# A recurrent-memory attention kernel: four streaming slots and 45 resident weight granules in place of five and 44

## The chip, the core and the metric

The kernel runs on one core of a Trainium2 chip. The metric is device time in microseconds (us) of one launch, as the median of several runs. Each weight that the kernel needs more than once has either to stay in SBUF, the on-chip memory of the core, or to be fetched again from HBM, the chip's main memory.

The engines are named as in the profile: PE (TensorE, matrix products), PEld (its weight loads), DVE (VectorE), ACT (ScalarE), POOL (GpSimd) and SP (SyncE, which here only issues transfers). DMA means the core's 16 transfer engines. "Granted clock" is the share of full speed that the chip let TensorE run at.

## The reference

The input `x` (2048 rows of 1024, bfloat16) is normalized by rows. The result is the sum of `x`, a recurrent attention layer, and a small routed layer:

```python
for s in range(64):                       # 2048 rows in segments of 32
    h = concatenate([mem, xn[32*s:32*s+32]])         # 8 memory rows + 32 rows
    q, k, v = h @ Wq, h @ Wk, h @ Wv                 # each 1024 -> 32 heads x 128
    p = softmax(where(mask, q @ k.T * 128**-0.5, -1e9))
    o = (p @ v) @ Wo                                 # 4096 -> 1024
    mem = o[:8]                                      # goes into the next segment
    outs.append(o[8:])
out = x + concatenate(outs) + B(xn)
```

`o` of a segment has 40 rows: the first 8 become the memory of the next one, so the 64 segments run strictly one after another. `B` scores all rows with one vector, takes the two best rows, sends only those through a gated layer (1024 to 3584 and back), and adds the result to these two rows.

## The kernel before

**Granules.** The four matrices Wq, Wk, Wv, Wo hold 32 MB in bfloat16, of which the kernel keeps only a part in SBUF. It cuts them into 64 granules of 128 x 2048 elements (512 KB): granules 0 to 47 are six phases of eight (`PHASES`: Q first half, K first half, Q second half, K second half, V first half, V second half; eight granules sum over the 1024 inputs), and granules 48 to 63 are Wo, two heads in each. Every segment uses all 64 in this order.

**Resident and streamed.** 44 granules (`N_RES`) are loaded once, in the first segment, and stay in SBUF (tiles `wres`). The other 20 are streamed: in the first segment from the input, and copied at the same time (`copy_block`, by POOL's queue) into a contiguous scratch array in HBM (`wsc`); in each of the 63 later segments they are fetched from there (`fetch`, L327 on SP's queue) into one of `N_SLOT` = 5 slots (tile `g`) that are used in turn. The streamed granules are 2, 5, 6, 9, 13, 17, 21, 25, 29, 33, 36, 39, 41, 44, 47, 50, 53, 56, 59, 62. Two are special: granule 6 (`KEPT_WHOLE`) lies in PSUM after the first segment and is never fetched again (ACT and DVE copy it back into small tiles in each segment), and of granule 25 (`KEPT_PART`) only the first half is fetched; the other half is copied from PSUM into its slot by two DVE copies (`kept_piece`, L354), which are hooked behind granules 17 and 18 in the order of DVE. So a later segment fetches 18 whole granules and one half.

**What starts a fetch.** SP takes its transfers in the order written. A fetch into a slot waits until PE has done the last matrix product that reads the granule five fetches earlier, which had the same slot. Landing is a second condition on PE's side: a product with a streamed granule waits until its fetch has landed. Nothing else paces the fetches.

**PE's order.** PE takes its products in the order written. For a granule of Q, K, V it does four products side by side (L661, tile `PSm`), for one of Wo eight (L713, tile `WO`). Each segment's 24 first rows (with the 8 memory rows) go through this main pass. The 8 rows that remain of each segment are gathered over four segments and go through the weights as a "left" pass of 32 rows (L644 and the `WL` products of L713): Q and K for the next group in segments j = 1 and 2 of a group of four, V in segment j = 0, Wo in segment j = 3 and partly the start of the next one. So a granule is read a second time in some of the segments, right behind the main product (in the second V phase of j = 0 the reads of its first granules wait until the fourth; in Wo of j = 3, those of granule 48 until granule 49), and its slot is free only then.

**Other paths.** Between the phases ACT copies a phase's sums out of PSUM (`XB`, `VM`), PE transposes them back (L515), DVE copies K's (`KT`, L525), and scores, softmax and the weighted sums follow at fixed places among the granules. After the last granule of a segment the eight memory rows are turned (`mem_to_st`) and the next segment starts.

**Start and end.** In the first segment SP loads granules, resident and streamed, and the tiles of `x` for the row statistics, about 14 granules ahead of PE. In the last segment every resident tile becomes free after its use, and SP fetches the 46 tiles of the routed layer into them and into the slots (`fetch_moe`, tiles `MW`), behind the last streamed fetch. Its products (L858, L871) end the kernel.

Of the kernel before, what the change touches and what calls it, by code (L numbers as in the profile page):

```python
# [14 lines left out]
PSUM = bass.MemoryType.PSUM  # L15
DRAM = bass.MemoryType.DRAM

N_RES = 44
N_SLOT = 5
KEPT_WHOLE = 6  # L20
KEPT_PART = 25
LEFT_OUT = 35
NEG = -30000.0

PHASES = [(0, 0), (1, 0), (0, 1), (1, 1), (2, 0), (2, 1)]
# [3 lines left out]
def kernel(  # L29
# [41 lines left out]


    NG = 64
    n_str = NG - N_RES
    streamed = [((2 * i + 1) * NG) // (2 * n_str + 2) for i in range(n_str + 1)]
    streamed.remove(LEFT_OUT)

    moved = {1: 2, 4: 5, 7: 9, 10: KEPT_WHOLE, 16: 17, 19: 21, 22: KEPT_PART, 25: 29, 28: 33, 32: 36, 38: 39}
    streamed = sorted(moved.get(g, g) for g in streamed)
    resident = [g for g in range(NG) if g not in streamed]  # L80

    def granule_dram(g):
# [13 lines left out]
    front = ctx.enter_context(tc.tile_pool(name="front", bufs=1, reuse_waits="tile"))  # L96
    wstream = ctx.enter_context(tc.tile_pool(name="wstream", bufs=N_SLOT))
    one = ctx.enter_context(tc.tile_pool(name="one", bufs=1, reuse_waits="tile"))
# [10 lines left out]
    def columns(g, s):  # L109
        if s > 0 and g == KEPT_WHOLE:  # L110
            return None
        return slice(0, 1024 if s > 0 and g == KEPT_PART else 2048)

# [190 lines left out]
    def new_stl(t):  # L304
# [10 lines left out]
    KEPT_COLS = {KEPT_WHOLE: {0: KEPT[0][:, 0:512], 1: KEPT[0][:, 512:1024], 2: KEPT[1][:, 0:512], 3: KEPT[1][:, 512:1024]},  # L315
                 KEPT_PART: {2: KEPT[2][:, 0:512], 3: KEPT[2][:, 512:1024]}}

    def fetch():
        if not flow:
            return  # L320
        s, g = flow.pop(0)
        t = wstream.tile([P, 2048], BF16, tag="g", name="g")
        c = columns(g, s)
        if s == 0:
            nc.sync.dma_start(out=granule_out(t, g), in_=granule_dram(g))
        elif c is not None:
            nc.sync.dma_start(out=t[:, c], in_=wsc[g][:, :])  # L327
        queued.append((g, t))
# [19 lines left out]
    def bring_back(c, copy):  # L348
        back[c] = one.tile([P, 512], BF16, tag=("bx", "bE", "kt", "bC")[c], name="BK")
        copy(out=back[c][:, :], in_=KEPT_COLS[KEPT_WHOLE][c])  # L350

    def kept_piece(g, c, copy):
        t = [t for q, t in queued if q == g][0]
        copy(out=t[:, 512 * c:512 * (c + 1)], in_=KEPT_COLS[g][c])  # L354
# [16 lines left out]
    def fetch_moe():  # L371
        while moe and free_homes:
            what = moe.pop(0)
            h = free_homes.pop(0)
            t = home(h, [P, 2048], BF16, "MW") if h >= 0 else wstream.tile([P, 2048], BF16, tag="g", name="g")
            if what[0] == "gu":
                _, w, kc, fh = what
                nc.sync.dma_start(out=t[:, 0:FH],
                                  in_=(B_w_gate, B_w_up)[w][kc * P:(kc + 1) * P, FH * fh:FH * (fh + 1)])
            else:  # L380
                nc.sync.dma_start(out=t.rearrange("p (a d) -> p a d", a=2),
                                  in_=B_w_down[2 * what[1] * P:(2 * what[1] + 2) * P, :].rearrange("(a p) d -> p a d", a=2))
            moe_tiles[what] = t
# [19 lines left out]
    for g in range(48):  # L403
        if g in streamed:
            n_q += 1
            if n_q < N_SLOT:
                fetch()
            continue
        if n_q >= N_SLOT:
            break  # L410
# [89 lines left out]
    for s in range(NSEG):  # L500
# [8 lines left out]
        def hook(p, kc, fn):  # L509
            hooks.setdefault((p, kc), []).append(fn)  # L510
# [112 lines left out]
        if s > 0:  # L623
            hook(0, 0, lambda: bring_back(3, nc.scalar.copy))
            hook(2, 1, lambda: kept_piece(KEPT_PART, 2, nc.vector.tensor_copy))
            hook(2, 2, lambda: kept_piece(KEPT_PART, 3, nc.vector.tensor_copy))
            hook(1, 5, turn_lx)
# [20 lines left out]
        for p, (mat, half) in enumerate(PHASES):  # L648
# [8 lines left out]
            for kc in range(KC):  # L657
                g = 8 * p + kc
# [140 lines left out]

    free_homes += [-1] * N_SLOT  # L800
    fetch_moe()
# [111 lines left out]
```

## Time and profile before

| what | value |
|---|---|
| median of 3 runs | 1981.58 us (1977.93 to 1991.66) |
| the profiled execution, its own time | 1977.82 us |
| its span, first to last instruction | 1976.2 us |
| PE busy | 1633.7 us (83%) |
| DMA moved | 712.43 MB, mean 361 GB/s |
| mean granted TensorE clock | 0.953 |

The profile page gives for each engine how long it was busy, then the span in 40 slices, the DMA queues, the chain of work that ended last, and groups of instructions. A "group" row names the line of the kernel, the engine, the operation, the tile written and the tiles read, the count, and what the engine waited for just before it. The view of windows gives the same busy times for stretches of the span that one chooses, with the mean granted clock, the share of time that the 16 DMA engines were busy, and the rate. The view of waits says which engine stood idle until what ended it: total us, number of times, longest one.

### The profile page before, as it was taken

What the parts mean: (1) busy time and instruction counts of PE and PEld (TensorE: products, weight loads), DVE (VectorE), ACT (ScalarE), POOL (GpSimd) and SP (SyncE); (2) the same over time, 40 slices, a digit from 0 to 9 for tenths busy, and PEclk for the clock granted to TensorE, in tenths of its full rate; (3) what the DMA queues carried; (4) which work ended last, traced back from release to release, by engine and by line L of the source; (5) the groups of instructions that cost most, each with busy time, mean ns of one, the idle gap of its engine ahead of it and who ended that gap; (6) DMA issues with size and microseconds to landing.
All of it is one profiled execution on the core that took longest, in us unless ns stands there. A gap on an engine that the chain in (4) does not pass through costs nothing.

```text
span 1976.2 us, 82904 instructions
## 1 busy us (share of the span) xinstructions
PE 1633.7 (83%) x36080; PEld 891.5 (45%) x36080; DVE 884.4 (45%) x2848; ACT 730.5 (37%) x1995; POOL 439.7 (22%) x882
## 2 busy tenths in 40 slices
PE   3558888988888898889898888888888898988863
PEld 1224544444454444445454544445444444544443
DVE  6724544454444434443453445444444544444430
ACT  1123343434334343433343444433434343343320
POOL 3201213112221312222121312222132122212110
PEclk8669999999999999999999999999999999999995
DMA  9999999999999999999999999999999999999998
GB/s 368 405 337 365 355 361 359 375 354 353 373 344 368 365 359 375 347 379 340 362 352 352 380 365 376 343 364 350 350 349 357 370 347 361 348 354 361 375 387 335
DMA packets 232124, 712.43 MB, mean 361 GB/s; under 512 B 39296, under 2 KB 53168, under 8 KB 231760
## 3 DMA queue, kind: packets, MB, share of 16 engines
q1 hardware_dynamic: 194384, 671.18, 91.5%
q0 software_dynamic: 28736, 28.09, 4.4%
q10 hardware_dynamic: 8640, 7.87, 1.1%
q8 instruction: 282, 4.62, 0.9%
q14 instruction: 82, 0.67, 0.1%
HBM read 694.32 MB, written 22.29 MB: 363 GB/s over the span
## 4 chain that ended last, share of the span: by engine, by line
DMA 47%; PE 40%; DVE 4%; ACT 3%; issue 3%; POOL 2%; SPq 1%; ACTq 0%; POOLq 0%; DVEq 0%
DMA g<-wsc 36%; PE PSm L661 18%; PE WO L713 7%; PE PSl L644 5%; DMA out_dram<-OL 4%; PE BT L515 3%; PE WL L713 2%; POOL out_dram L792 1%; PE BT L465 1%; DMA MW<-in_B_w_gate_dram 1%; DVE XR L227 1%; DMA MW<-in_B_w_up_dram 1%; ACT QT L520 1%; DMA ql_d<-XBl 1%; DMA g<-in_A_Wq_dram 1%
## 5 line engine op out<-in xcount | busy, mean ns | idle before, releaser
L661 PE MATMUL PSm<-wres,ST 128*32 128x512 bf16 x8448 | 723.0, 387 | 15.7 <-DVE ST L282 5.4
L661 PEld LDWEIGHTS <-ST 128*32 128x32 bf16 x12288 | 325.7, 96 | 420.9 <-issue 195.1
L661 PE MATMUL PSm<-g,ST 128*32 128x512 bf16 x3588 | 367.6, 389 | 108.5 <-DMA g<-wsc 89.0
L677 ACT CAST XB<-PSm 128x512 bf16<-128x512 f32 x256 | 150.5, 588 | 306.5 <-PE PSm L661 306.5
L713 PEld LDWEIGHTS <-OT 128*32 128x32 bf16 x8192 | 205.3, 98 | 114.7 <-issue 90.9
L713 PE MATMUL WO<-wres,OT 128*32 128x256 bf16 x5632 | 237.0, 282 | 22.3 <-issue 13.8
L458 POOL DMA_DIRECT2D LX<-ql_d x63 | 33.5, 532 | 910.8 <-DVE OTL L592 325.9
L644 PE MATMUL PSl<-wres,STL 128*32 128x512 bf16 x2112 | 203.1, 391 | 13.4 <-ACT VL L701 12.4
L525 DVE COPY KT<-BT 128x512 bf16<-128x512 bf16 x128 | 53.3, 416 | 321.0 <-issue 163.0
L252 POOL DMA_DIRECT2D XN<-in_A_x_dram x256 | 128.4, 507 | 244.1 <-DMA out_dram<-XN 126.7
L778 POOL DMA_DIRECT2D out_dram<-XN x256 | 129.1, 513 | 233.0 <-DVE XN L776 227.4
L713 PE MATMUL WO<-g,OT 128*32 128x256 bf16 x2560 | 133.6, 283 | 41.3 <-DMA g<-wsc 29.0
L644 PEld LDWEIGHTS <-STL 128*32 128x32 bf16 x3072 | 85.1, 98 | 74.5 <-issue 26.3
L515 PE MATMUL BT<-IDENT,XB 128*128 128x128 bf16 x1024 | 102.0, 222 | 17.9 <-ACT XB L677 16.3
L697 ACT CAST VM<-PSm 128x512 bf16<-128x512 f32 x128 | 79.2, 619 | 100.5 <-PE PSm L661 100.5
L515 PEld LDWEIGHTS <-XB 128*128 128x128 bf16 x1024 | 58.4, 98 | 124.1 <-ACT XB L677 83.5
L354 DVE COPY g<-KEPT 128x512 bf16<-128x512 bf16 x126 | 47.6, 419 | 143.7 <-PE PSm L661 85.9
L542 DVE TENSOR_TENSOR BS<-BS,CT 128x96 f32<-128x96 f32 (+1 forms) x256 | 59.6, 233 | 101.0 <-PE BS L535 96.6
L583 PEld LDWEIGHTS <-VM 32*128 32x128 bf16 x2048 | 69.6, 92 | 77.9 <-issue 72.2
L520 ACT COPY QT<-BT 128x512 bf16<-128x512 bf16 x128 | 75.2, 588 | 71.1 <-PE BT L515 64.8
L552 ACT ACTIVATE BS<-BS 128x320 f32<-128x320 f32 x128 | 54.1, 423 | 116.9 <-DVE BS L548 116.8
L644 PE MATMUL PSl<-g,STL 128*32 128x512 bf16 x900 | 93.2, 391 | 0.0
(171 smaller groups left out, 2435.2 us busy)
## 6 DMA issues: line engine op xcount, KB each, us to landing
g<-wsc SPq DMA_DIRECT2D x1134, 512.0 KB, 6.0
g<-wsc SPq DMA_DIRECT2D x63, 256.0 KB, 5.5
LX<-ql_d POOLq DMA_DIRECT2D x63, 128.0 KB, 6.1
MW<-in_B_w_gate_dram SPq DMA_DIRECT2D x16, 448.0 KB, 9.2
MW<-in_B_w_up_dram SPq DMA_DIRECT2D x16, 448.0 KB, 9.0
wres<-in_A_Wk_dram SPq DMA_DIRECT2D x12, 512.0 KB, 12.3
MW<-in_B_w_down_dram SPq DMA_DIRECT2D x12, 512.0 KB, 10.4
wres<-in_A_Wq_dram SPq DMA_DIRECT2D x11, 512.0 KB, 11.4
```

Source lines behind the costliest of these rows:

```text
L252: nc.gpsimd.dma_start(out=XN[32 * g:32 * g + XM, :], in_=x2[s * SEG:s * SEG + XM, 256 * g:256 * (g + 1)])
L515: nc.tensor.transpose(out=PTq[:, il, :, :].rearrange("p j r -> p (j r)"), in_=XB[:, il * P:(il + 1) * P], identity=IDENT[:, :])
L520: nc.scalar.copy(out=QT[half][:, :, :], in_=pv)
L542: nc.vector.tensor_tensor(out=S4, in0=S4, in1=m, op=ALU.add)
L552: nc.scalar.activation(out=S8, in_=S8, func=ACTF.Exp, scale=SCALE)
L583: nc.tensor.matmul(o, lhsT=VM[half][q0:q0 + 32, il * P:(il + 1) * P], rhs=PTm[q0:q0 + 32, il, 0:NK], start=True, stop=False, tile_position ...
L644: nc.tensor.matmul(PSl[32 * jq:32 * jq + 32, :], lhsT=STL[:, g % KC, :], rhs=part(Gv, jq), start=first_, stop=last_, tile_position=(0, 32 ...
L661: nc.tensor.matmul(PSm[32 * jq:32 * jq + 32, :], lhsT=ST[:, kc, :], rhs=part(Gv, jq), start=(kc == 0), stop=(kc == KC - 1), tile_position= ...
L677: nc.scalar.copy(out=XB[:, :], in_=PSm[:, :])
L697: nc.scalar.copy(out=VM[half][:, :], in_=PSm[:, :])
L713: nc.tensor.matmul(PS[32 * g:32 * g + 32, 0:256], lhsT=lhs(h), rhs=Gv[:, D * hs + 256 * g:D * hs + 256 * (g + 1)], start=False, stop=(last ...
L778: nc.gpsimd.dma_start(out=out2[s * SEG:s * SEG + XM, 256 * g:256 * (g + 1)], in_=OB[32 * g:32 * g + XM, :])
```

## The change

The kernel keeps 45 granules resident in place of 44 and streams 19 in place of 20. The room for the additional resident granule is that of a slot: there are four slots in place of five, so a fetch now waits for the granule four fetches earlier. A later segment fetches 17 whole granules and one half.

The list of streamed granules is written out in place of the formula. It becomes 2, 4, 6, 9, 13, 17, 21, 24, 29, 34, 36, 39, 42, 45, 48, 51, 55, 59, 62: 5 gives way to 4, 25 to 24, 33 to 34, 41, 44, 47, 50, 53, 56 to 42, 45, 48, 51, 55. The granule that is kept in part in PSUM is 24 in place of 25. Granule 48, the first one of Wo, is now streamed. Everything else in the file is the same; lines behind the list move up by three.

```diff
-N_RES = 44
-N_SLOT = 5
+N_RES = 45
+N_SLOT = 4
 KEPT_WHOLE = 6
-KEPT_PART = 25
-LEFT_OUT = 35
+KEPT_PART = 24
...
     NG = 64
-    n_str = NG - N_RES
-    streamed = [((2 * i + 1) * NG) // (2 * n_str + 2) for i in range(n_str + 1)]
-    streamed.remove(LEFT_OUT)
-
-    moved = {1: 2, 4: 5, 7: 9, 10: KEPT_WHOLE, 16: 17, 19: 21, 22: KEPT_PART, 25: 29, 28: 33, 32: 36, 38: 39}
-    streamed = sorted(moved.get(g, g) for g in streamed)
+
+    streamed = [2, 4, KEPT_WHOLE, 9, 13, 17, 21, KEPT_PART, 29, 34, 36, 39, 42, 45, 48, 51, 55, 59, 62]
+    assert len(streamed) == NG - N_RES
+    n_str = len(streamed)
     resident = [g for g in range(NG) if g not in streamed]
```

## The prediction

> **What bounds the kernel now.** I read the page first: span, engines, DMA queues, the chain that ended last and the DMA issues.
>
> ```profile
> span 1976.2 us, 82904 instructions
> PE 1633.7 (83%) x36080; PEld 891.5 (45%) x36080; DVE 884.4 (45%) x2848; ACT 730.5 (37%) x1995; POOL 439.7 (22%) x882
> ...
> DMA  9999999999999999999999999999999999999998
> ...
> q1 hardware_dynamic: 194384, 671.18, 91.5%
> ...
> DMA g<-wsc 36%; PE PSm L661 18%; PE WO L713 7%; PE PSl L644 5%; DMA out_dram<-OL 4%; PE BT L515 3%; PE WL L713 2%; POOL out_dram L792 1%; PE BT L465 1%; DMA MW<-in_B_w_gate_dram 1%; DVE XR L227 1%; DMA MW<-in_B_w_up_dram 1%; ACT QT L520 1%; DMA ql_d<-XBl 1%; DMA g<-in_A_Wq_dram 1%
> ...
> g<-wsc SPq DMA_DIRECT2D x1134, 512.0 KB, 6.0
> g<-wsc SPq DMA_DIRECT2D x63, 256.0 KB, 5.5
> ```
>
> The reader is to see two busy resources side by side: the DMA engines are at nine tenths or more nearly everywhere, PE is busy for 83%, and the chain changes between PE and the streamed fetches (1134 whole, 63 half: 18 and 1 in each of 63 segments). The windows and the waits of PE say how near the two are.
>
> ```profile
> 155.00:1908.00 1753.00, 1526.39 (x34105) 832.41 (x34104) 790.21 (x2598) 696.64 (x1913) 400.41 (x796) 0.98 0.98 360
> 0.00:105.00 105.00, 46.84 (x578) 20.59 (x578) 71.65 (x180) 14.46 (x35) 27.98 (x64) 0.77 1.00 388
> 1908.00:1976.00 68.00, 28.64 (x863) 23.48 (x862) 5.52 (x22) 7.23 (x17) 6.62 (x12) 0.65 0.91 350
> ```
>
> ```profile
> PE PSm L661 <- DMA g<-wsc: 89.0, 153, 1.6
> PE WO L713 <- DMA g<-wsc: 29.0, 67, 1.7
> ```
>
> ```profile
> L705 PE MATMUL WO<-XS,IDENT x64: 269/269/393, 104.9 to 1908.5; 128*128 128x256 bf16 x64
> ```
>
> The last three figures of a window are granted clock, DMA share and GB/s. L705 runs once a segment, so it marks the segments; the long window holds 62 of them, 1753 / 62 = 28.3 us each. In it DMA works for 0.98 x 28.3 = 27.7 us a segment. PE stands for streamed data for 89.0 + 29.0 = 118 us in 220 waits, 0.54 us in each and 118 / 63 = 1.9 us a segment; without them a segment would take 26.4 us. **The bound is the stream**, with PE and what it waits for otherwise only 1.3 us behind.
>
> The four kinds of segment differ. I took one group of four without any fall of the clock (1.00), whose sum, 113.3 us, is near four average segments (113.1), cut at the marks of L705, and its waits on streamed data: none in the first stretch, then those below.
>
> ```profile
> 549.13:580.82 31.69, 27.42 (x666) 16.48 (x666) 13.69 (x48) 11.08 (x33) 9.60 (x18) 1.00 0.93 327
> 580.82:607.58 26.76, 24.28 (x540) 12.72 (x540) 12.05 (x38) 12.33 (x35) 4.73 (x10) 1.00 0.99 360
> 607.58:635.10 27.52, 24.37 (x538) 12.85 (x537) 12.44 (x41) 11.50 (x33) 4.71 (x10) 1.00 1.00 369
> 635.10:662.46 27.36, 21.69 (x474) 11.48 (x473) 12.66 (x43) 10.31 (x31) 7.17 (x14) 1.00 1.01 385
> ```
>
> Second stretch:
>
> ```profile
> PE PSm L661 <- DMA g<-wsc: 0.9, 2, 0.5
> ```
>
> Third, then fourth:
>
> ```profile
> PE WO L713 <- DMA g<-wsc: 1.4, 3, 0.9
> PE PSm L661 <- DMA g<-wsc: 1.2, 3, 0.5
> ```
>
> ```profile
> PE PSm L661 <- DMA g<-wsc: 2.2, 4, 0.7
> PE WO L713 <- DMA g<-wsc: 1.7, 3, 1.2
> ```
>
> DMA work (length x share) is 29.5, 26.5, 27.5, 27.6 us; the length without these waits is 31.7, 25.9, 24.9, 23.5 us. The larger of each pair adds up to 31.7 + 26.5 + 27.5 + 27.6 = 113.3, the measured sum. So in this group five slots carry the stream to its bound: no time is lost beside the larger of the two.
>
> **The change part by part.** *One whole fetch less in each of 63 segments.* Queue q1 moved 671.18 MB in 91.5% of the span, 1808 us, so a granule (0.524 MB) costs 1808 / 671.18 x 0.524 = 1.41 us of all engines. It takes 63 x 1.41 = 89 us of DMA work out, and once the 0.5 MB copy into `wsc`, 1.4 us at the same rate, in the first 105 us (DMA 1.00). Not all 89 us come back, because PE is next. In the group above DMA work falls to 28.1, 25.1, 26.1, 26.2, the other side stays, and the larger of each pair adds up to 31.7 + 25.9 + 26.1 + 26.2 = 109.9: 3.4 to 3.5 us a group, 0.87 a segment, **55 us** in all, if four slots carried the stream as well as five.
>
> *One slot less.* A fetch starts one streamed granule later.
>
> ```profile
> L327 SPq DMA_DIRECT2D g<-wsc x1197: 319/320/1618, 119.0 to 1908.4; - x200
> ...
> DMA to landing us min/median/max: 3.2/6.0/10.6
> ```
>
> A slot turns in 5 x 28.3 / 19 = 7.45 us: 6.0 in flight, 1.45 landed and not yet released. With four slots and 18 fetches it has 4 x T / 18, at 28.3 us 6.3 us. If the flight stayed at 6.0 and the hold fell to about 0.5 (a product, 0.38, and SP), T would be 18 x 6.5 / 4 = 29.3 us, against 27.4 with full gain. But most of the flight is queueing behind the kernel's own fetches: the fastest of 1197 landed in 3.2 us, and half a granule less moves the median by 0.5 us (5.5 against 6.0), so one whole granule less ahead should take about 1.0 off: 5.0 in flight, which an even flow bears easily (18 x 5.5 / 4 = 24.8 us). What the slot guarded against is an uneven flow: the reserve over the shortest turn (3.2 + 0.5 = 3.7 us, 2.6 granules at 1.41) falls from 2.4 granules to 1.4. Bounds: nothing at the one end; at the other 29.3 - 27.4 = 1.9 us a segment. I take one more average wait in each segment, 0.54 us, **34 us** in all, since the waits are the nearest row for a buffer run dry: now 3.5 a segment with a reserve of 2.4.
>
> [...]
>
> *The new places.* Counts of PE, DVE and ACT instructions stay; the products only read other tiles. In segments that end a group, granule 48's slot comes free only at granule 49, at most about 0.4 us later (26.4 / 64 a granule) in 16 segments: bounds 0 and 7 us, taken at 0, since its successor 62 is 14 granules away. In the second V phase 42 replaces 41 among the granules whose release waits for the fourth; that is no worse.
>
> *The kept half.* The two copies into the slot now wait for granule 9's release in place of 5's, and K's copy is queued behind them on DVE, with the scores (L533) behind that.
>
> ```profile
> L354 DVE COPY g<-KEPT x126: 411/420/426, 136.2 to 1891.7; 128x512 bf16<-128x512 bf16 x126
> ```
>
> ```profile
> PE BS L533 <- DVE KT L525: 6.8, 19, 0.6
> ```
>
> From granule 9 to 19, where K's copy is due, PE needs 10 x 0.41 = 4 us, against 0.84 us for both copies. I take 0; if this cover were gone, 63 times the longest wait, 0.6, is 38 us.
>
> *Start and end.* Fetch 9 goes out behind more resident loads; in the first 105 us DMA is at 1.00, so order changes nothing but who waits: 0. The end is the routed layer's 46 tiles, in 45 homes and a slot, behind the last streamed fetch:
>
> ```profile
> 1899.16 6.87 DMA g<-wsc
> ...
> 1912.19 9.26 DMA MW<-in_B_w_gate_dram
> ...
> 1970.07 0.62 PE YP L871 x8
> ```
>
> The same bytes follow the same event: 0.
>
> **Sum**: -55 + 34 - 1 = -22 us. The profiled execution, 1977.8 us (span and 1.6 around it), goes to 1956; on the median, 1981.6, which is 3.8 above it, to **1959**, 1.1% faster.
>
> **The rivals.** *A, the lost slot costs nothing*: 55 + 1 us gained, 1925. For it: the group above loses nothing with five, and fetches land sooner with fewer bytes queued. Against: the reserve nearly halves. *B, the flight does not shrink*, and the stream is bound by four slots: T = 29.3 us, 63 x (29.3 - 28.3) = +63 us, 2044. It decides where flight and hold exceed 4 x 28.3 / 18 = 6.29 us, that is, a median landing of 5.8. For it: landings up to 10.6 us. Against: DMA is at 0.98, so flight is mostly queue. In part (landing near 5.9) it gives 1990 to 2000. *C, even*: two more average waits a segment (68 us), 1994, or 1.6 of them, 1980. *D, other waits take the place of the removed ones*:
>
> ```profile
> PE BT L515 <- ACT XB L677: 16.3, 26, 1.2
> PE PSl L644 <- ACT VL L701: 12.4, 13, 2.4
> ```
>
> Where PE comes sooner, ACT's copies end later than it: at twice these rows 29 us less gain, beside the 34, which is 1988. *E, the clock*: the shallower buffer bunches waits, as here after three in a row:
>
> ```profile
> 999.70:1006.50 6.80, 6.80 (x122) 3.17 (x122) 3.44 (x16) 2.03 (x10) 0.00 (x0) 0.50 0.98 377
> ```
>
> A mean of 0.98 is 4% of the stage, 70 us, at half speed; were it 8%, 35 us of PE time would go, half of it on the path where PE binds: 1959 + 18 = 1977. [...]
>
> That the change doesn't do what it says is unlikely: the count of fetches follows from the list.
>
> **How the numbers follow.** Forecast 0.44 (1940 to 1970); A 0.24 (1915 to 1940); C, D and E together 0.18 (1970 to 1995); B 0.14 (1995 to 2044). A change of 1% (20 us) is about what a measurement of this kernel tells from none, its runs lying between 1978 and 1992. Faster by over 1% (under 1962): all of A and two thirds of the forecast, 0.53. Slower by over 1% (over 2001): most of B, 0.13, and 0.02 of the rest. Same 0.32. The range leaves out the low part of A and B's: 1922 to 1996.
>
> **What would show it.** Fetches 1071 whole and 63 half; q1 near 638 MB; median landing near 5.0 us, where 5.8 or more is B; DMA share near 0.94 in the long window, 27.9 us a segment; PE's waits on `g<-wsc` still about 100 us, where 50 is A; waits on L677 and L701 near 29 us, where twice is D; clock 0.98, where 0.96 is E; L533 on L525 still under 10 us. The prediction is wrong above all if the price of the slot is not near 0.5 us a segment.

## The result and the profile after

The changed kernel takes **2057.9 us** (median; 2043.6 to 2071.5), the kernel before beside it 1982.9 us: a ratio of 1.039, with a 95% interval of 1.035 to 1.043. It is 75 us slower, where 22 us faster was forecast.

The page of the changed kernel, profiled in an execution of 2050.0 us; lines of the kernel count three less than before:

```profile
span 2048.4 us, 82702 instructions
PE 1641.9 (80%) x36080; PEld 894.6 (44%) x36080; DVE 886.1 (43%) x2848; ACT 730.1 (36%) x1995; POOL 439.6 (21%) x881
...
GB/s 368 405 336 343 334 340 318 317 340 328 315 318 336 317 318 336 323 339 313 343 323 343 334 326 328 308 330 322 329 324 326 332 318 327 330 338 323 332 339 336
...
q1 hardware_dynamic: 185312, 638.14, 87.5%
...
g<-wsc SPq DMA_DIRECT2D x1071, 512.0 KB, 5.5
g<-wsc SPq DMA_DIRECT2D x63, 256.0 KB, 4.4
```

The marks of the segments, the windows, and the waits of PE:

```profile
L702 PE MATMUL WO<-XS,IDENT x64: 269/269/394, 104.2 to 1979.5; 128*128 128x256 bf16 x64
```

```profile
0.00:105.00 105.00, 48.72 (x578) 20.73 (x579) 70.45 (x179) 15.02 (x36) 27.79 (x63) 0.75 1.00 387
...
155.00:1980.00 1825.00, 1531.64 (x34043) 834.04 (x34041) 791.02 (x2594) 696.39 (x1913) 400.43 (x796) 0.98 0.94 328
1980.00:2048.00 68.00, 27.94 (x858) 23.05 (x846) 5.33 (x22) 6.26 (x13) 6.63 (x12) 0.63 0.91 347
```

```profile
PE PSm L658 <- DMA g<-wsc: 177.0, 250, 2.6
PE WO L710 <- DMA g<-wsc: 48.8, 78, 2.7
...
PE BT L512 <- ACT XB L674: 14.1, 15, 0.9
...
PE PSl L641 <- ACT VL L698: 1.4, 2, 1.1
PE BS L530 <- DVE KT L522: 1.0, 3, 0.5
```

The time from issue to landing of the fetches of L324:

```profile
DMA to landing us min/median/max: 2.8/5.5/7.7
```

SP's own waits for the landing of the granule that had the slot, after and then before:

```profile
SPq L324 <- DMA g<-wsc: 511.8, 708, 3.0
```

```profile
SPq L327 <- DMA g<-wsc: 301.2, 515, 2.6
```

The reader is to see that the change did what it says: 1071 whole fetches and 63 half ones, 638 MB on q1 in place of 671. Start (105 us, DMA 1.00) and end (68 us) are as before. All of the loss lies in the 63 steps from segment to segment: 1979.5 - 104.2 = 1875 us against 1908.5 - 104.9 = 1804 us. The first step holds the first fetches and is longer in both, so below a segment is taken from the long windows, which hold 62 of them: 1825 / 62 = 29.4 us against 1753 / 62 = 28.3. There the rate of the transfers fell from 360 to 328 GB/s, and PE waits 226 us for streamed data in place of 118. When SP comes to a fetch, the granule that had the slot has more often not even landed: it waits for that 708 times in 1134 fetches, before 515 times in 1197. Fewer bytes are to be fetched, and they come more slowly still.

The DMA share alone would have hidden this: it fell only from 0.98 to 0.94 while the rate fell by 9%. On q1, the queue of SP's transfers, a MB now takes 0.875 x 2048.4 / 638.14 = 2.81 us of all engines; before it took 2.69.

### The profile page after: what moved, and what is told of

It is laid out like the page before. It is cut to its first block, busy times and chain, and to the rows that moved or that the text cites. A ratio compares the mean times of both kernels' runs of the same rounds, so it can differ in the third digit from the quotient of the medians.

```text
span 2048.4 us, 82702 instructions
## 1 busy us (share of the span) xinstructions
PE 1641.9 (80%) x36080; PEld 894.6 (44%) x36080; DVE 886.1 (43%) x2848; ACT 730.1 (36%) x1995; POOL 439.6 (21%) x881
## 3 DMA queue, kind: packets, MB, share of 16 engines
q1 hardware_dynamic: 185312, 638.14, 87.5%
## 5 line engine op out<-in xcount | busy, mean ns | idle before, releaser
L658 PE MATMUL PSm<-wres,ST 128*32 128x512 bf16 x8704 | 766.3, 391 | 7.8 <-DVE ST L279 5.4
L658 PEld LDWEIGHTS <-ST 128*32 128x32 bf16 x12288 | 331.5, 97 | 510.5 <-issue 288.1
L658 PE MATMUL PSm<-g,ST 128*32 128x512 bf16 x3332 | 341.4, 393 | 202.4 <-DMA g<-wsc 177.0
L641 PE MATMUL PSl<-wres,STL 128*32 128x512 bf16 x2176 | 208.6, 393 | 2.0 <-ACT VL L698 1.4
L522 DVE COPY KT<-BT 128x512 bf16<-128x512 bf16 x128 | 53.8, 420 | 240.2 <-issue 119.2
L512 PE MATMUL BT<-IDENT,XB 128*128 128x128 bf16 x1024 | 102.2, 223 | 15.6 <-ACT XB L674 14.1
L580 PEld LDWEIGHTS <-VM 32*128 32x128 bf16 x2048 | 64.7, 91 | 85.7 <-issue 73.3
L587 ACT CAST OT<-BS 128x128 bf16<-128x128 f32 x128 | 34.1, 266 | 169.5 <-PE BT L582 122.1
```

Of the source, the lines that this page charges most:

```text
L512: nc.tensor.transpose(out=PTq[:, il, :, :].rearrange("p j r -> p (j r)"), in_=XB[:, il * P:(il + 1) * P], identity=IDENT[:, :])
L580: nc.tensor.matmul(o, lhsT=VM[half][q0:q0 + 32, il * P:(il + 1) * P], rhs=PTm[q0:q0 + 32, il, 0:NK], start=True, stop=False, tile_position ...
L641: nc.tensor.matmul(PSl[32 * jq:32 * jq + 32, :], lhsT=STL[:, g % KC, :], rhs=part(Gv, jq), start=first_, stop=last_, tile_position=(0, 32 ...
L658: nc.tensor.matmul(PSm[32 * jq:32 * jq + 32, :], lhsT=ST[:, kc, :], rhs=part(Gv, jq), start=(kc == 0), stop=(kc == KC - 1), tile_position= ...
```

## The experiments

Three theories: (1) the lost slot is the price, since fewer bytes are under way; in an even flow already (1a), or only as a reserve for an uneven one (1b). (2) The new places of the streamed granules are the price. (3) The tiles lie at other addresses and their packets are slower. Each ratio below is to the kernel before on the same chip; GB/s is the rate in the long window, as above.

| kernel | streamed | slots | median us | ratio, 95% interval | GB/s |
|---|---|---|---|---|---|
| before | 20 | 5 | 1982.9 | 1 | 360 |
| changed | 19 | 4 | 2057.9 | 1.039 [1.035, 1.043] | 328 |
| e1 old places | 20 | 4 | 2149.2 | 1.090 [1.084, 1.095] | 331 |
| e2 new places | 19 | 5 | 1911.9 | 0.968 [0.963, 0.972] | 353 |
| e3 new places | 19 | 6 | 1877.9 | 0.950 [0.945, 0.955] | 358 |
| e5 old places, one less | 19 | 4 | 2061.6 | 1.045 [1.042, 1.049] | 326 |
| e6 new places, one more | 20 | 5 | 1998.9 | 1.011 [1.007, 1.016] | 354 |
| e4 one more streamed, one more slot | 21 | 6 | 1942.4 | 0.985 [0.983, 0.988] | 387 |
| e7 two more of both | 22 | 7 | 2023.0 | 1.028 [1.026, 1.030] | 388 |
| e8 changed, in halves | 19 | 8 halves | 2057.5 | 1.044 [1.041, 1.046] | 327 |
| e9 old, in halves | 20 | 10 halves | 2013.1 | 1.022 [1.021, 1.024] | 353 |

### The slot alone

```diff
-N_SLOT = 5
+N_SLOT = 4
```

(on the kernel before, with its own list)

> The old list of 20 streamed granules and 44 resident ones, with four slots in place of five: the slot alone. The changed kernel took 75 us more in all, where one granule less streamed should give 55 us, so theory 1 (the lost slot is the price, 2.0 us a segment) expects 1983 + 130 = about 2110 us, a DMA share near 0.93 in the middle and over 300 us of waits of PE on streamed data. Theory 2 (the new places are the price) expects about 1985 us. Theory 3 (the tiles lie at other addresses in memory and their packets are slower) expects about 1985 too, since the scratch array is as before.

Measured: 2149.2 us, 173 us more than the kernel before in the same comparison (1975.8). Window and waits:

```profile
155.00:2060.00 1905.00, 1565.37 (x34061) 849.38 (x34063) 787.90 (x2583) 697.01 (x1909) 400.55 (x796) 0.97 0.95 331
```

```profile
PE PSm L658 <- DMA g<-wsc: 212.0, 290, 3.1
PE WO L710 <- DMA g<-wsc: 64.8, 109, 2.4
```

With everything else as before, the slot costs 9%, and the stream runs at 331 GB/s, as in the changed kernel. Theories 2 and 3 cannot give this: places and scratch array are the old ones. (What lies behind the slots in SBUF moves by one slot; the stream by itself, below, shows the rate fall with the very same slots, four of them in use and five.) It is even more than theory 1 had put (130), though PE's waits on the stream (277 us) and the DMA share (0.95) moved less than expected (over 300, and 0.93).

### The lighter stream, with five and with six slots

The room for the slots comes from resident granules that aren't loaded, whose products read a neighbour's tile (so these two kernels serve for timing only):

```diff
-N_SLOT = 4
+N_SLOT = 5
...
+    shared = {37: 35}
+
     def load_resident(g):
+        if g in shared:
+            res_tiles[g] = res_tiles[shared[g]]
+            return
...
-            if g in resident:
+            if g in resident and g not in shared:
                 free_homes.append(g)
```

(six slots: `shared = {37: 35, 46: 44}`)

> The new list of 19, with five slots: granule 37 is not loaded and its products read the tile of granule 35 (so these products are other ones, of the same size), which makes the room for the fifth slot. Theory 1 expects the gain of the lighter stream without the price of the slot: 1983 - 56 = about 1927 us (1900 to 1945). Theories 2 and 3 expect what the changed kernel showed, about 2050 us.

> As the run with five slots and the new list, with six: granule 46 is not loaded either and its products read the tile of granule 44. Theory 1 expects a smaller step than from four to five, since PE without waits on streamed data (118 us fewer) is the floor, near 1865: about 1895 us. Theories 2 and 3: still about 2050 us.

Measured: 1911.9 us and 1877.9 us against 1975.8, near theory 1's numbers (1927, 1895), far from those of 2 and 3. With five slots:

```profile
155.00:1840.00 1685.00, 1498.78 (x33924) 824.10 (x33924) 783.66 (x2577) 689.96 (x1899) 400.04 (x795) 0.98 0.97 353
```

```profile
PE PSm L663 <- DMA g<-wsc: 50.3, 90, 2.2
...
PE WO L715 <- DMA g<-wsc: 14.8, 25, 1.9
```

With six:

```profile
155.00:1820.00 1665.00, 1490.08 (x34034) 823.49 (x34030) 787.66 (x2589) 692.30 (x1909) 400.45 (x796) 0.99 0.98 358
```

```profile
PE WO L585 <- ACT OTL L594: 27.3, 34, 1.8
...
PE BT L517 <- ACT XB L679: 17.3, 32, 1.2
PE PSl L646 <- ACT VL L703: 17.0, 13, 3.7
...
PE PSm L663 <- DMA g<-wsc: 10.9, 24, 1.0
```

One granule less streamed is worth 64 us with five slots. The price of the fifth slot is the difference of the changed kernel and e2: 0.0715 of 1976 us, 141 us, or 2.2 us a segment. Six slots also show PE's own pace: with only 11 us left of waits of PE on the stream, a segment takes 1665 / 62 = 26.9 us, 26.7 without these waits, where the prediction had 26.4.

### The stream by itself

```python
for k in range(n - 1):                     # per stage, with n slots
    send()
for k in range(90):
    if len(sent) < 90:
        send()                             # 512 KB, SP's queue, into slot len(sent) % n
    for jq in range(4):                    # read at once by four products
        nc.tensor.matmul(PS[32 * jq:32 * jq + 32, :], lhsT=ST[:, k % KC, :],
                         rhs=sent[k][:, 512 * jq:512 * (jq + 1)], ...)
```

> The stream by itself: 90 fetches of 512 KB from 18 scratch arrays in each of seven stages with 5, 4, 3, 6, 2, 4 and 5 slots, each granule read by four products at once; no attention, no norm, no routed layer, the output is a copy of x. If the price of the slot is the time of flight in an even flow (theory 1a), four slots give one granule per (5.5 + 0.5) / 4 = 1.5 us and five one per 1.3 us. If an even flow bears four slots and only an uneven one does not (theory 1b), both give 1.3 to 1.4 us, three slots perhaps 1.4, and only two slots are clearly slower, near (3.2 + 0.5) / 2 = 1.85 us.

Measured, the middles of the stages with 5, 4, 3, 6 and 2 slots (columns: length, PE, PEld, DVE, POOL, granted clock, DMA share, GB/s):

```profile
60.00:150.00 90.00, 42.81 (x280) 7.70 (x276) 0.00 (x0) 0.00 (x0) 1.00 1.02 406
180.00:280.00 100.00, 41.54 (x272) 7.41 (x268) 0.00 (x0) 0.00 (x0) 1.00 0.97 352
320.00:440.00 120.00, 41.40 (x268) 7.44 (x268) 0.00 (x0) 0.00 (x0) 1.00 0.87 294
470.00:560.00 90.00, 43.27 (x280) 7.79 (x280) 0.00 (x0) 0.00 (x0) 1.00 1.03 410
600.00:770.00 170.00, 43.27 (x280) 7.80 (x280) 0.00 (x0) 0.00 (x0) 1.00 0.69 215
```

A granule of 0.524 MB takes 2.4, 1.8, 1.49, 1.29, 1.28 us with 2, 3, 4, 5 and 6 slots. Theory 1a holds: the even flow alone loses 13% from five to four slots, and six add nothing. The later stages with four and five slots repeated 353 and 403 GB/s. The share falls much less than the rate: 0.97 at 352 GB/s, though the engines can do 410. A share near 1 is no proof that the engines are at their rate. (Each stage ran once, but for the two that were repeated.)

### Ways to get more out of four slots

> The stream by itself again, 90 granules a stage: four slots as before; four slots with SP and ACT issuing in turn; four slots with each granule as two transfers of 256 KB into the same slot; eight half slots of 256 KB, each released after its own two products; four and five slots with each granule read four times over, which holds a slot about 1.3 us longer. If the bytes in circulation and the time of a turn set the rate (theory 1a): 1.49 us for the first three, eight halves slightly under it, near 1.45, as a half is held for less, four held slots near (5.3 + 0.7 + 1.0) / 4 = 1.75 and five held near 1.45. If it is a limit of SP's queue or of the size of a transfer, two queues or two transfers are clearly under 1.49 us.

```python
q = queues[k % len(queues)]        # SP, or SP and ACT in turn
if own:                            # half slots of their own, W = 1024
    q.dma_start(out=t[:, :], in_=wsc[(k // 2) % NGR][:, W * (k % 2):W * (k % 2 + 1)])
elif halves:                       # two transfers into one slot
    for c in range(2):
        q.dma_start(out=t[:, 1024 * c:1024 * (c + 1)], in_=wsc[k % NGR][:, 1024 * c:1024 * (c + 1)])
else:
    q.dma_start(out=t[:, :], in_=wsc[k % NGR][:, :])
```

The middles of the stages in order: four slots; SP and ACT in turn; two transfers to a slot; eight half slots; four and five slots held longer:

```profile
60.00:165.00 105.00, 42.69 (x280) 7.64 (x276) 0.00 (x0) 0.00 (x0) 1.00 0.97 348
205.00:295.00 90.00, 36.71 (x240) 6.64 (x240) 0.00 (x0) 0.00 (x0) 1.00 0.95 348
320.00:420.00 100.00, 79.68 (x264) 13.67 (x264) 0.00 (x0) 0.00 (x0) 1.00 0.99 347
460.00:570.00 110.00, 97.05 (x320) 16.57 (x318) 0.00 (x0) 0.00 (x0) 1.00 1.04 380
595.00:705.00 110.00, 73.91 (x1116) 23.86 (x1108) 0.00 (x0) 0.00 (x0) 0.98 0.94 333
740.00:840.00 100.00, 74.19 (x1124) 24.05 (x1120) 0.00 (x0) 0.00 (x0) 0.98 0.99 368
```

Neither a second queue nor smaller transfers change the rate (348 and 347 GB/s against 348); it isn't a limit of SP's queue or of a transfer's size. Holding the slots longer lowers it, less than expected (333 GB/s is 1.57 us, expected 1.75; 368 is 1.42, expected 1.45). Halves that come free by themselves raise it, more than expected (1.38 us, expected 1.45).

In the kernel the same halves were tried:

```diff
-    wstream = ctx.enter_context(tc.tile_pool(name="wstream", bufs=N_SLOT))
+    wstream = ctx.enter_context(tc.tile_pool(name="wstream", bufs=2 * N_SLOT))
...
-        t = wstream.tile([P, 2048], BF16, tag="g", name="g")
+        t = two_halves()        # two tiles [P, 1024], one transfer each
```

> The changed kernel with the room of its four slots cut into eight halves of 256 KB: a granule is two transfers into two tiles, and each half comes free after its own last product. Same bytes, same room, same places. In the stream by itself this raised the rate from 348 to 379 GB/s, over half the way to five slots (406). If the price of the slot is the rate that the bytes in circulation allow (theory 1a), about half of the 141 us comes back: 1985 (1960 to 2010). If the price is the reserve for an uneven flow (theory 1b), the reserve in bytes is the same and the kernel stays within 1% of the changed one, 2055.

> The old kernel with its five slots cut into ten halves. By the rate in an even flow there is little left to gain (406 against 410 GB/s), so theory 1a gives 0 to 20 us: 1955 to 1976. If a finer release helps an uneven flow too, 1930 to 1955. It is slower if only eight transfers can be under way at a time (SP's transfers wait for one another's completion in a ring of eight), since eight halves are four granules: 1990 to 2010.

Measured: 2057.5 us, the time of the changed kernel, and 2013.1 us, slower than the kernel before (1969.2 there). The eight halves:

```profile
155.00:1985.00 1830.00, 1596.49 (x34079) 840.50 (x34079) 788.92 (x2589) 695.46 (x1912) 400.85 (x796) 0.99 0.96 327
```

```profile
L339 SPq DMA_DIRECT2D g<-wsc x2205: 319/382/2867, 122.9 to 1989.1; - x184
...
DMA to landing us min/median/max: 2.6/5.2/16.6
```

```profile
PE PSm L678 <- DMA g<-wsc: 133.9, 275, 2.3
PE WO L730 <- DMA g<-wsc: 33.0, 69, 1.4
```

This is against my expectation from theory 1a; of the two, the expectation from theory 1b is the one that was met. The 18 granules of a segment take 36 half slots (one half is copied and not fetched), so a half slot turns in 8 x 29.5 / 36 = 6.6 us, and a whole slot of the changed kernel in 4 x 29.4 / 18 = 6.5 us. By the traces the halves are on average 5.1 us in flight and held for 1.5, the whole slots 5.5 and 1.0. What the halves gain in flight goes into the hold. That two halves of a granule wait for the same place in PE's order is the likely reason; it is argued, not shown. PE's waits on the stream fall to 167 us from 226, but its busy time in the window rises as much, to 1596 us from 1532: the second pair of a granule's four products starts 0.26 us after the first on average (0.01 in the changed kernel), so PE waits between the pairs in place of before them.

For the ten halves, the trace shows the limit of eight transfers that was named beforehand. The fetches report their landing on eight semaphores in turn, and though a slot comes round only every ten, no fetch goes out before the one eight earlier has landed; of the 1734 for which the trace tells that landing, 41% go out within 0.15 us of it, against 4% with eight halves. That this limit makes all of the 44 us is not shown. SP's waits for it:

```profile
SPq L339 <- DMA g<-wsc: 351.2, 943, 2.4
```

In the run with eight halves this row is 69 us. With whole slots the row means something else, the landing of the granule that had the slot before, and can't be compared with these two.

### The places alone

```diff
# e5, on the changed kernel
-    streamed = [2, 4, KEPT_WHOLE, 9, 13, 17, 21, KEPT_PART, 29, 34, 36, 39, 42, 45, 48, 51, 55, 59, 62]
+    streamed = [2, 5, KEPT_WHOLE, 9, 13, 17, 21, KEPT_PART, 29, 33, 36, 39, 44, 47, 50, 53, 56, 59, 62]
# and KEPT_PART = 25
# e6, on the changed kernel, with N_RES = 44 and N_SLOT = 5
+    streamed = [2, 4, KEPT_WHOLE, 9, 13, 17, 21, KEPT_PART, 29, 34, 36, 39, 42, 45, 48, 51, 53, 55, 59, 62]
```

> The old list without granule 41, so 19 streamed and 45 resident, with four slots: the changed kernel but for the places. If the places matter little (theory 1), within 1.5% of the changed kernel, 2055 (2025 to 2085). If the new places are what four slots need, it is slower, above 2085; if they are part of the loss (theory 2), under 2025.

> The new list with granule 53 added, 20 streamed, 44 resident, five slots: the old kernel but for the places. Theory 1: within 1% of the old kernel, 1976 (1956 to 1996). Theory 2: slower by more than that.

Measured: 2061.6 us, a ratio of 1.045 against 1.039 of the changed kernel, so with four slots the old places are 0.6% slower if anything (the two intervals allow up to 1.4%); and 1998.9 us, 1.1% slower than the old places with five slots, just outside of what I had allowed theory 1. Theory 2 has a small part at most: the new places are a little worse with five slots and not worse with four. The rate with four slots and the old places:

```profile
155.00:1985.00 1830.00, 1544.56 (x33948) 843.95 (x33940) 788.27 (x2583) 693.36 (x1902) 400.27 (x796) 0.97 0.94 326
```

Three kernels with four slots, two lists and two amounts of data run at 326 to 331 GB/s. With four slots, it is the slots that set the rate.

### The other direction

```diff
# e4, on the kernel before
-N_RES = 44
-N_SLOT = 5
+N_RES = 43
+N_SLOT = 6
# e7
+N_RES = 42
+N_SLOT = 7
```

(the lists are written out, in the two expectations, so the places differ too)

> One step the other way: 43 resident granules, 21 streamed (2, 5, 6, 9, 12, 15, 18, 21, 25, 29, 33, 36, 39, 41, 44, 47, 50, 53, 56, 59, 62), six slots. Theory 1: the sixth slot is worth 34 us (five to six with 19 streamed), one more streamed granule costs 64 us (19 to 20 with five slots), so 1976 + 30 = about 2005 us, and the old kernel is at the best size. If depth is worth more with a heavier stream, as four to five was (173 us with 20, 141 with 19), it may be near 1980.

> One step further than 21 streamed and six slots: 42 resident, 22 streamed (2, 4, 6, 8, 11, 14, 17, 20, 23, 25, 29, 33, 36, 39, 41, 44, 47, 50, 53, 56, 59, 62), seven slots. A streamed granule costs about 32 us at six slots (1878 to 1942 for two). The rate of an even flow gains nothing over six slots, so theory 1a expects 1942 + 32 = 1974; if the reserve for an uneven flow still grows in worth (theory 1b), 1940 or less.

Measured: 1942.4 us, 1.5% faster than the kernel before (0.983 to 0.988) and 5% faster than the changed one: **of the sizes tried, the best is one step the other way**. My sum of 2005 was 3% off; depth is worth more under a heavier stream, as from four to five slots (173 us with 20 streamed, 141 with 19). With 22 and seven it is 2023.0 us, not 1974. Windows of the two:

```profile
155.00:1870.00 1715.00, 1515.62 (x34123) 832.01 (x34123) 790.04 (x2598) 697.26 (x1919) 401.92 (x796) 0.99 1.01 387
```

```profile
155.00:1950.00 1795.00, 1539.15 (x34100) 838.57 (x34095) 791.20 (x2599) 698.90 (x1916) 400.75 (x796) 0.98 1.01 388
```

Both run at 387 to 388 GB/s, not far from the 410 of the stream by itself, in a kernel that holds 360 with five slots. From there a further slot adds no rate, and a further streamed granule costs about its time: 1.3 us of transfers a segment, 63 times, is 82 us; measured 81 by the medians, 84 by the two ratios. I had taken 32 us, from a comparison of kernels in which PE was the bound.

## Why the prediction was wrong

**The time, the sign and the range: wrong.** 2058 us lies above the range, and above the end of rival B (2044).

- *Bytes and counts: right.* 1071 and 63 fetches, 638 MB.
- *The gain of the lighter stream, if four slots carried it as well as five (55 us and 1): right.* e2 shows it with five slots: 64 us.
- *The price of the slot (0.54 us a segment, 34 us): the step that failed.* It is 2.2 us a segment, 141 us (e2 against the changed kernel), and 173 us with 20 streamed (e1). Even my far bound, 1.9, was under it. Two readings led there. First, "5.0 in flight, which an even flow bears easily (18 x 5.5 / 4 = 24.8 us)": the flight fell only to 5.5, the slots were held 1.0 on average and not 0.5, and the stream by itself shows that four slots carry an even flow more slowly: 352 GB/s in place of 406, one granule in 1.49 us, which is 18 x 1.49 = 26.8 us a segment and not 24.8. I had the flight shorten by 1.0 us for each granule less in the queue, from a row of half granules; from five to four it shortened by 0.5. Second, **the DMA share of 0.98 was read as engines at their bound**, so that most of the flight had to be queue. But 360 GB/s at 0.98 was no bound: six slots reach 387. The kernel before was itself short of bytes under way.
- *Rival B: the right mechanism, with wrong terms.* I had put its point at a median landing of 5.8 us. What counts is flight and hold together, which have to exceed 6.29 us by its own formula; by the trace they are 5.5 + 1.0 = 6.5. That B's own sum, 6.0 + 0.5, is 6.5 too, and its 2044 us so near, is luck: the flight did shrink, and the hold was twice what it had.
- *The group of four in which "no time is lost beside the larger of the two"* took the engines' busy time for work that had to be done. With few fetches under way a part of that time is packets that take longer (see the last section), so the sum can come out right without a bound; this is argued.
- *PE at 26.4 us without waits on the stream: a little low.* It is 26.7 (e3), as other waits come up, which is the mechanism of rival D. But most of it is a row that D didn't name (PE on ACT's `OTL`, 27.3 us, 1.8 before); D's own two rows are 34 us there in place of 29, and in the changed kernel they fell to 14.1 and 1.4.
- *The new places, put at nothing: nearly right.* They cost 1.1% with five slots (e6), and nothing that shows with four (e5). Granule 48 has no row of its own.
- *The kept half, start, end, clock: right.* L530 waits 1.0 us on L522, the clock is 0.98, start and end are unchanged.
- *The fastest landing, 3.2 us, as the flight when little is queued: too short.* With two slots in the stream by itself I took (3.2 + 0.5) / 2 = 1.85 us a granule; measured 2.4, as the median landing there is 4.2 us. In the changed kernel the fastest landing is 2.8 us and the median 5.5. What binds four slots is a flight that stays at 5.5 us; how much of it is a fixed part, no run here shows.

How the 2.2 us divide stays open in part. As an estimate, with four slots and 352 GB/s the 9.7 MB of a segment (328 GB/s x 29.4 us) would take 27.4 us, and with five and 406, 23.8. PE asks for 26.7, and with five slots a segment took 1685 / 62 = 27.2 us (e2). So an even flow through four slots is as slow as the rest of the kernel, where five slots had 3 us to spare, but by itself it explains only 0.2 of the 2.2 us. The rest must be the unevenness, now without that room (theory 1b). This is by subtraction, not shown; the halves, which helped the even flow and not the kernel, speak for it.

## What to carry to other kernels

Before a buffer of a stream is given up, count bytes under way: compare the rate reached, not the busy share of the transfer engines, with the best rate that the same core reaches elsewhere in the trace (here 388 GB/s in the first 105 us against 360 in the middle was the hint). A slot's price is then flight and hold, over the number of slots, against the pace that the rest of the kernel asks for. And the flight need not shorten as much as the queue when a slot goes: here the median went from 6.0 to 5.5 us, 8%, with one slot in five gone. The exchange of slots against resident data is worth a try in both directions: here the best size tried lay on the other side.

## What I had not expected of the hardware

The lone stream of 512 KB fetches needed five slots for its rate: 215, 294, 352, 406, 410 GB/s with two to six slots, while the share of busy time goes 0.69, 0.87, 0.97, 1.02, 1.03. So a MB costs 3.2 us of the engines' busy time with two slots and 2.5 with six. In the traces the packets of 4 KB themselves took longer when few fetches were under way: 210, 192, 180, 164, 163 ns on average with two to six slots, with the median at 159 to 161 throughout, and 184 ns in the changed kernel, 176 before and 168 in e4. What the long ones wait for, no run here shows. By the bytes that the slots of the stream hold together, the rate is 215 GB/s with 1.0 MB, 352 with 2.1 and 410 with 3.1. These 410 GB/s of one core lie above the 360 of the kernel before, so its 360 was not the most that one core reaches here.
